# w_out in four pieces and a listed order anew: a linear-attention and gated feed-forward kernel on one core

## The chip, the cores and the metric

The kernel runs on one NeuronCore of a Trainium2 chip. Its engines are TensorE (PE in the profile, its weight loads PEld), VectorE (DVE), ScalarE (ACT), GpSimd (POOL) and SyncE (SP). Each works through its own list of instructions in order, and semaphores make one wait for another. SP and POOL also issue DMAs; all of them run on the core's 16 DMA engines. The metric is device time in microseconds of one execution, as a median over runs.

## The reference

Eight batches of eight heads, 576 tokens, head width 64, then a gated feed-forward over the 4608 tokens:

```python
q_s = exp(q - max(q, -1));  q_s = q_s / (sum(q_s, -1) + 1e-09)     # over the head width
k_s = exp(k - max(k, 2));   k_s = k_s / (sum(k_s, 2) + 1e-09)      # over the tokens
kv  = einsum('bhsd,bhse->bhde', k_s, v)
x   = einsum('bhsd,bhde->bhse', q_s, kv)     # then (4608, 512): tokens x heads * width
out = ((x @ w1) * (x @ w2)) @ w3 @ w_out     # 512 -> 1024, 1024 -> 1024, 1024 -> 512
```

q, k, v, the weights and the output are float32 in DRAM; the matmuls take float16.

## The kernel before

**The fold.** Nothing stands between w3 and w_out, so the kernel first forms W3O = w3 @ w_out (1024 x 512) and later multiplies by that alone. It does this in eight blocks of 128 rows of w3, `ft` 0 to 7 (`fold`, lines 411 to 442). For each block PE transposes eight 128 x 128 tiles (`w3t`), ACT or DVE copies them out of PSUM (`w3T`), PE multiplies them with w_out in eight matmuls of 512 columns that accumulate in one PSUM bank (`pf`), and ACT or DVE scales the sum into W3O (`W3O`). The eight matmuls are cut into as many steps as w_out has pieces: step `pf.ft.h` takes piece `h` alone, so it can start when that piece has landed.

**The attention** of batch b (`attention`). For k: the maximum over the tokens (`kmx`, `cb`), its subtraction (`ksub`, in two halves of the heads), the exponential (`kexp`), the product with v (`kv`, on PE) and its division by the sums (`kv2`). v of later batches is first cast (`vc`). For q, in two parts of the tokens: maximum (`qmx`), subtraction (`qsub`), exponential (`qexp`), sum (`qsm`), a small constant added (`qeps`), reciprocal (`qrc`), product (`qn`). Then q is transposed, for batches 0 and 1 on PE (`qt`, copied out by `qT`), for the others by a transposing DMA on SP (`qd`). PE multiplies it with kv (`xm`, `xt` for the last 64 tokens), and `xs` and `xts` copy the result out as x.

**The feed-forward** of chunk c (`chunk`): eight pairs of PE steps, `up.1` with w2 and `up.0` with w1; `bs` copies the first product out, `ab` multiplies the two on DVE; then four `down` steps with W3O, their copies `os` and the stores `st` on SP. Chunk 8 holds the last 64 tokens of all batches.

**The order.** Every step is named, and `ORDER` (lines 80 to 150) lists all of them. `Plan.run` (lines 51 to 75) emits them in that order, so each engine's and each queue's order is the list's, restricted to it. `PICKS` says which engine takes a step that has a choice; its names hold for the batches from 3 on together (`qeps_3_1`). Some DVE and POOL steps share a port; for the first `LINKED` places of the list the kernel adds a wait wherever the holder of that port changes engine. `FILL` puts matmuls on zeros ahead of a step: 17 at the beginning and 16 ahead of `pf.4.0`.

**The loads.** SP loads q of batch 0 (`HW`), and later what batches from 2 on need. POOL issues the loads in `LOADS` (lines 198 to 202): the weights, which are cast to float16 on the way, and k, v and q of the first batches. A load on POOL's queue waits until the load eight places ahead of it has landed (`load`, line 400). w3 comes in six pieces (`ROWS`: rows of blocks 0, 1, 2, 3, 4-5, 6-7), w1 and w2 in four (`COLS`). The number of w_out's pieces is this line (239), used by `side` and `fold`:

```python
    WOS = 2
```

Of the kernel before, what the change touches and what calls it, by code (L numbers as in the profile page):

```python
# [201 lines left out]
]  # L202
# [673 lines left out]
```

## Time and profile before

| | |
|---|---|
| median of three runs | 243.53 us (243.4 to 244.03) |
| the profiled execution, its own time | 243.27 us |
| its span in the trace | 241.5 us |
| PE busy | 234.5 us, 97% of the span |
| DVE, ACT, POOL busy | 170.8, 123.4, 124.0 us |
| PE's waits for DMAs | 2.2 us, in four places, all before 25.4 us |
| matmuls on zeros | 33, 10.0 us |
| DMA | 45.66 MB, a mean of 189 GB/s |

The span runs from the first to the last instruction in the trace; the execution's own time adds what lies around it. Times inside the trace are microseconds from the span's start. In a group's line an arrow `a<-b` says that a is written from b; `<-DMA v` behind a wait says that it was ended by a DMA that wrote v. In the timeline of an engine the first number is the start, the second the duration of a merged run of like instructions, and brackets hold the idle time before it.

### The profile page before, as it was taken

Reading aid. Unit: us, or ns where it says so; the run is one execution under the profiler, and the core shown is the slowest. Engines: PE = TensorE matmul, PEld = TensorE weight load, DVE = VectorE, ACT = ScalarE, POOL = GpSimd, SP = SyncE. Lnnn points to the kernel's source line nnn. Section 1 sums busy time; section 2 is a strip of 40 time slices with the busy share of each in tenths; the row PEclk is TensorE's granted clock in tenths of the full one; section 3 lists DMA queues with packets and bytes.
Section 4 is the critical chain, followed back from the end, with each engine's and each line's share of the span. In section 5 each row is a group of like instructions: output and inputs, shape, how many; then the busy total and the mean of one; then the engine's idle time right before and its main releaser. Section 6 shows DMA issues by size and latency. Waiting matters only on the chain.

```text
span 241.5 us, 4827 instructions
## 1 busy us (share of the span) xinstructions
PE 234.5 (97%) x1917; PEld 114.6 (47%) x1917; DVE 170.8 (71%) x293; ACT 123.4 (51%) x194; POOL 124.0 (51%) x79
## 2 busy tenths in 40 slices
...
PEclk9999999999999999999999999999999999999999
...
GB/s 209 310 209 250 305 302 200 249 370 356 399 388 160 274 1 114 380 341 83 206 400 124 248 401 281 153 0 35 165 76 3 49 38 133 0 0 0 88 132 130
DMA packets 37894, 45.66 MB, mean 189 GB/s; under 512 B 15984, under 2 KB 22384, under 8 KB 37872
## 3 DMA queue, kind: packets, MB, share of 16 engines
...
q0 software_dynamic: 7792, 11.14, 21.0%
...
q14 instruction: 7, 0.06, 0.1%
...
## 4 chain that ended last, share of the span: by engine, by line
PE 88%; DMA 7%; POOL 2%; issue 1%; ACT 0%; POOLq 0%
PE pab L735 52%; PE po L757 23%; DMA v<-in_v_dram 7%; PE po L772 3%; PE po L427 3%; PE pkv L515 2%; PE xm L621 2%; POOL w L377 1%; PE w3t L415 1%; PE xt L621 1%; PE pkv L524 1%; POOL wosb L377 0%; PE qtp L595 0%; POOL q L377 0%; POOL k L377 0%
## 5 line engine op out<-in xcount | busy, mean ns | idle before, releaser
L750 DVE TENSOR_TENSOR ab<-pab,bsb 128x512 f16<-128x512 f32 x72 | 48.8, 684 | 28.4 <-PE pab L735 24.8
L735 PE MATMUL pab<-x,w1sb 128*128 128x512 f16 (+1 forms) x288 | 65.9, 356 | 0.0
L735 PE MATMUL pab<-x,w2sb 128*128 128x512 f16 (+1 forms) x288 | 65.8, 356 | 0.0
L298 ACT CAST bsb<-pab 128x512 f16<-128x512 f32 x59 | 34.6, 586 | 52.0 <-PE pab L735 51.7
L757 PE MATMUL po<-W3O,ab 128*128 128x512 f16 x256 | 59.5, 380 | 0.0
L490 POOL TENSOR_TENSOR k<-k,cb 128x1152 f32<-128x1152 f32 x15 | 39.2, 2629 | 20.3 <-DVE cb L486 19.1
L735 PEld LDWEIGHTS <-w2sb 128*128 128x128 f16 x320 | 30.7, 98 | 30.6 <-issue 0.2
L735 PEld LDWEIGHTS <-w1sb 128*128 128x128 f16 x320 | 30.6, 98 | 29.6 <-issue 0.2
L580 POOL TENSOR_TENSOR en<-eq,qr 128x1280 f16<-128x1280 f16 (+1 forms) x15 | 32.1, 2141 | 15.3 <-ACT x L302 6.3
L757 PEld LDWEIGHTS <-ab 128*128 128x128 f16 x256 | 24.0, 98 | 29.2 <-issue 2.7
L548 POOL TENSOR_TENSOR q<-q,qm 128x1024 f32<-128x1024 f32 (+1 forms) x14 | 29.7, 2126 | 8.6 <-DVE qm L543 6.3
L298 ACT COPY osb<-po 128x512 f32<-128x512 f32 (+1 forms) x29 | 16.6, 572 | 28.5 <-PE po L757 22.6
L459 DVE TENSOR_REDUCE km<-k 128x128 f32<-128x1152 f32 x12 | 25.4, 2115 | 0.0
L543 DVE TENSOR_REDUCE qm<-q 128x20 f32<-128x1280 f32 (+1 forms) x16 | 21.4, 1344 | 4.1 <-DMA q<-in_q_dram 4.1
L302 ACT ACTIVATE x<-xm 128x512 f16<-128x512 f32 x30 | 16.5, 595 | 10.0 <-PE xm L621 9.8
L561 DVE TENSOR_REDUCE qr<-eq 128x20 f32<-128x1280 f16 (+1 forms) x16 | 21.3, 1330 | 0.4 <-ACT eq L556 0.4
L556 ACT ACTIVATE eq<-q 128x1280 f16<-128x1280 f32 (+1 forms) x16 | 18.6, 1165 | 5.6 <-POOL q L548 2.9
L498 ACT ACTIVATE ek<-k 128x1152 f16<-128x1152 f32 x16 | 18.5, 1164 | 2.5 <-POOL k L490 2.5
L298 DVE CAST bsb<-pab 128x512 f16<-128x512 f32 x13 | 9.0, 690 | 13.4 <-PE pab L735 13.3
L427 PE MATMUL po<-wosb,w3T 128*128 128x512 f16 x64 | 15.3, 379 | 1.2 <-DMA wosb<-in_moe_w_out_dram 1.2
L325 PE MATMUL po<-zero 128*128 128x512 f16 x33 | 10.0, 470 | 1.6 <-DVE zero L320 1.6
L427 PEld LDWEIGHTS <-w3T 128*128 128x128 f16 x64 | 5.8, 98 | 7.8 <-ACT w3T L298 1.2
...
## 6 DMA issues: line engine op xcount, KB each, us to landing
...
v<-in_v_dram POOLq DMA_DIRECT2D x2, 576.0 KB, 14.6
...
wosb<-in_moe_w_out_dram POOLq DMA_DIRECT2D x2, 512.0 KB, 12.1
```

The source lines that it names most:

```text
L298: return [(nc.scalar.copy if eng == "ACT" else engine[eng].tensor_copy)(out=out, in_=in_)]
L427: nc.tensor.matmul(st["pf", ft], lhsT=st["w3T", ft][:, gt, :], rhs=wosb[:, gt, :], start=(gt == 0), stop=(gt == N_FT - 1))
L459: dve.tensor_reduce(out=st["km", b][:, two(hp), :], in_=kb[:, two(hp), :, :].rearrange("p h j d -> p h d j"), axis=AX.X, op=ALU.max)
L490: return [engine[eng].tensor_tensor(out=kb[:, two(hp), :, :], in0=kb[:, two(hp), :, :], in1=st["cb", b][:, two(hp), None, :].broadcast_to( ...
L543: dve.tensor_reduce(out=st["qm", b][:, :, j], in_=qb[:, :, j, :], axis=AX.X, op=ALU.max)
L548: return [engine[eng].tensor_tensor(out=qb[:, :, j, :], in0=qb[:, :, j, :], in1=st["qm", b][:, :, j, None].broadcast_to([P, HH, n, D]), op ...
L556: nc.scalar.activation(out=st["eq", b, p], in_=qb[:, :, j, :], func=AF.Exp)
L561: dve.tensor_reduce(out=st["qr", b][:, :, slice(*PARTS[p])], in_=st["eq", b, p], axis=AX.X, op=ALU.add)
L580: return [engine[eng].tensor_tensor(out=st["en", b][:, j, :, :].rearrange("p j h d -> p h j d"), in0=st["eq", b, p], in1=st["qr", b][:, :, ...
L735: nc.tensor.matmul(st["p", one, c, sub, u][:, a * (t1 - t0):(a + 1) * (t1 - t0)], lhsT=w[:, ct, fb * P:(fb + 1) * P], rhs=x()[:, ct, t0:t1 ...
L750: dve.tensor_tensor(out=st["ab", c][:, nf * u:nf * u + nf, t0:t1], in0=cut(st["p", 0, c, sub, u]), in1=cut(st["bsb", c, sub, u]), op=ALU.mult)
L757: nc.tensor.matmul(st["po", c, tb], lhsT=st["ab", c][:, ft, tb * P:(tb + 1) * P], rhs=W3O[:, ft, :], start=(ft == 0), stop=(ft == N_FT - 1))
```

## The change

w_out is loaded in four pieces instead of two, and the fold's eight matmuls of a block become four steps of two. In `LOADS` the pieces 1 and 0 stand ahead of k of batch 0, the pieces 2 and 3 behind it; w3's piece with blocks 6-7 (`w3.5`) moves from behind v of batch 0 to ahead of q of batch 1. The dummy matmuls ahead of `pf.4.0` go from 16 to 8. `ORDER` and `PICKS` are newly listed: up to chunk 4 the steps stand in another order, from there on in the old one, and some steps change engine. `LINKED` goes from 191 to 211, since the list has more steps ahead of the same point. The computation is the same. Of `ORDER` the diff shows the places that follow: the beginning up to the first `up` steps, and the stretch from `kv.2` to the transposes of batches 2 and 3.

```diff
-LINKED = 191
+LINKED = 211
 ORDER = """
-q.0.1 q.0.0 w3.4 k.0 wo.0 wo.1 ident w3.3 w3.0 qmx.0.1 w3.1 q.1.0 qsub.0.1 qexp.0.1 qmx.0.0 w3t.5
-v.0 w3t.4 qsm.0.1 w3T.4 qsub.0.0 qeps.0.1 w3.5 qexp.0.0 kmx.0.0 w3T.5 w3.2 pf.4.0 qrc.0.1 cb.0
-qn.0.1 pf.5.0 pf.4.1 qsm.0.0 k.1 qt.0.8 W3O.4 w2.0 w3t.3 qeps.0.0 ksub.0.1 pf.5.1 w3T.3 w1.0
-qt.0.16 w3t.0 qrc.0.0 qT.0.8 qn.0.0 pf.3.0 kexp.0.1 pf.3.1 w3T.0 ksub.0.0 w3t.1 W3O.5 qt.0.0
-w3T.1 W3O.3 pf.0.0 qmx.1.0 pf.1.0 kexp.0.0 qT.0.0 pf.0.1 qT.0.16 qsub.1.0 k.2 kv.0 w2.1 W3O.0
-qexp.1.0 pf.1.1 w1.1 kv2.0 w3t.7 w2.2 qsm.1.0 w3t.6 w3T.7 xm.0.1 w1.2 w3t.2 xs.0.1.0 w3T.6 pf.7.0
-W3O.1 xs.0.1.1 pf.7.1 qeps.1.0 pf.6.0 w3T.2 W3O.7 v.1 kmx.1.0 xm.0.0 pf.6.1 xs.0.0.1 xs.0.0.0
-pf.2.0 w2.3 up.1.0.0.0 w1.3 qrc.1.0 up.0.0.0.0 cb.1 bs.0.0.0 qn.1.0 up.1.0.0.1 up.0.0.0.1
-bs.0.0.1 ab.0.0.0 ksub.1.0 qt.1.0 kmx.2.0 pf.2.1 qT.1.0 up.1.0.0.2 W3O.2 xt.0 bs.0.0.2 q.1.1
...
-up.0.1.0.0 ab.0.0.7 qsub.1.1 kexp.2.1 up.1.1.0.1 qmx.2.1 bs.1.0.0 up.0.1.0.1 bs.1.0.1 ab.1.0.0
-down.0.0 qsub.2.1 qexp.1.1 qmx.2.0 vc.2.0 ab.1.0.1 q.3 up.1.1.0.2 v.3 qsm.1.1 vc.2.1 up.0.1.0.2
-k.4 qexp.2.1 up.1.1.0.3 qsub.2.0 os.0.0 qsm.2.1 up.0.1.0.3 qeps.1.1 bs.1.0.2 kv.2 qrc.1.1
-qexp.2.0 ab.1.0.2 down.0.1 qn.1.1 kv2.2 bs.1.0.3 q.4 st.0.0 ab.1.0.3 down.0.2 os.0.1 qmx.3.1
-st.0.1 qt.1.8 os.0.2 qeps.2.1 qrc.2.1 qt.1.16 qsub.3.1 down.0.3 qsm.2.0 qT.1.8 st.0.2 qT.1.16
-qmx.3.0 xm.1.1 down.1.0 xs.1.1.0 qn.2.1 kmx.3.1 xs.1.1.1 up.1.1.1.0 vc.3.0 qeps.2.0 up.0.1.1.0
-qexp.3.1 qd.2.1 qrc.2.0 kmx.3.0 qn.2.0 xt.1 up.1.1.1.1 os.0.3 up.0.1.1.1 bs.1.1.0 xts.1.0
-qsub.3.0 qd.2.0 up.1.1.1.2 xts.1.1 bs.1.1.1 qsm.3.1 ab.1.1.0 os.1.0 down.1.1 bs.1.1.2 ab.1.1.1
-st.1.0 up.0.1.1.2 os.1.1 qmx.4.1 up.1.1.1.3 v.4 st.1.1 ab.1.1.2 up.0.1.1.3 bs.1.1.3 qeps.3.1
-st.0.3 xm.2.0 vc.3.1 ab.1.1.3 down.1.2 xs.2.0.1 cb.3 xs.2.0.0 qsub.4.1 qexp.3.0 xm.2.1 down.1.3
-xs.2.1.0 qrc.3.1 xs.2.1.1 qsm.3.0 ksub.3.1 qexp.4.1 up.1.2.0.0 up.0.2.0.0 qeps.3.0 bs.2.0.0
...
+q.0.1 q.0.0 w3.4 wo.1 wo.0 k.0 wo.2 wo.3 w3.3 qmx.0.1 ident qsub.0.1 qmx.0.0 w3t.4 w3.0 qexp.0.1
+w3t.5 qsub.0.0 w3T.5 qsm.0.1 w3T.4 w3.1 qeps.0.1 qrc.0.1 w3.5 qexp.0.0 qn.0.1 pf.4.0 q.1.0 pf.5.0
+qsm.0.0 qt.0.16 pf.5.1 v.0 qt.0.8 pf.4.1 kmx.0.0 qeps.0.0 qT.0.8 pf.5.2 w3.2 pf.4.2 k.1 pf.5.3
+pf.4.3 W3O.5 qrc.0.0 W3O.4 cb.0 w3t.3 qn.0.0 w3T.3 w3t.0 qT.0.16 pf.3.0 w2.0 w3T.0 ksub.0.1
+pf.3.1 w3t.1 w1.0 pf.3.2 ksub.0.0 pf.3.3 pf.0.0 W3O.3 qt.0.0 w3T.1 pf.0.1 qT.0.0 pf.0.2 kexp.0.1
+pf.0.3 w3t.7 qmx.1.0 pf.1.0 w3T.7 pf.1.1 pf.1.2 W3O.0 kexp.0.0 pf.1.3 qsub.1.0 w3t.6 pf.7.0 k.2
+kv.0 W3O.1 qexp.1.0 w2.1 w1.1 pf.7.1 w3T.6 kv2.0 pf.7.2 w2.2 w3t.2 qsm.1.0 xm.0.1 w1.2 pf.7.3
+xs.0.1.1 pf.6.0 qeps.1.0 xs.0.1.0 w3T.2 pf.6.1 v.1 pf.6.2 W3O.7 kmx.1.0 xm.0.0 pf.2.0 xs.0.0.0
+pf.2.1 w2.3 xs.0.0.1 pf.2.2 pf.6.3 pf.2.3 w1.3 W3O.6 up.1.0.0.0 qrc.1.0 W3O.2 cb.1 qn.1.0
...
+qmx.1.1 bs.0.0.7 up.1.1.0.0 ab.0.0.7 up.0.1.0.0 qsub.1.1 bs.1.0.0 qmx.2.1 kexp.2.0 up.1.1.0.1
+down.0.0 bs.1.0.1 qmx.2.0 qsub.2.1 qexp.1.1 ab.1.0.0 up.0.1.0.1 os.0.0 down.0.1 ab.1.0.1 st.0.0
+vc.2.1 qexp.2.1 qsm.1.1 q.3 qsub.2.0 up.1.1.0.2 kexp.2.1 v.3 qsm.2.1 up.0.1.0.2 os.0.1 k.4
+up.1.1.0.3 vc.2.0 qexp.2.0 kmx.3.0 st.0.1 down.0.2 bs.1.0.2 q.4 qeps.2.1 bs.1.0.3 qeps.1.1
+qrc.1.1 kv.2 os.0.2 qn.1.1 ab.1.0.2 up.0.1.0.3 qrc.2.1 kv2.2 down.0.3 ab.1.0.3 qt.1.8 qn.2.1
+qmx.3.1 qt.1.16 os.0.3 down.1.0 qT.1.8 kmx.3.1 qT.1.16 qsub.3.1 qd.2.1 xm.1.1 down.1.1 xs.1.1.1
+qsm.2.0 xs.1.1.0 qexp.3.1 qeps.2.0 up.1.1.1.0 qrc.2.0 qmx.3.0 qn.2.0 up.0.1.1.0 bs.1.1.0 qsm.3.1
+up.1.1.1.1 os.1.1 vc.3.1 xt.1 qd.2.0 up.0.1.1.1 xts.1.0 ab.1.1.0 bs.1.1.1 qsub.3.0 up.1.1.1.2
+xts.1.1 st.1.1 ab.1.1.1 up.0.1.1.2 qmx.4.1 bs.1.1.2 st.0.3 os.1.0 up.1.1.1.3 ab.1.1.2 st.1.0
+up.0.1.1.3 qsub.4.1 bs.1.1.3 qeps.3.1 xm.2.0 ab.1.1.3 st.0.2 down.1.2 xs.2.0.0 qrc.3.1 xs.2.0.1
+cb.3 v.4 qexp.3.0 xm.2.1 down.1.3 xs.2.1.1 xs.2.1.0 qsm.3.0 ksub.3.0 qexp.4.1 up.1.2.0.0 kmx.4.0
+up.0.2.0.0 qeps.3.0 bs.2.0.0 up.1.2.0.1 ksub.3.1 ab.2.0.0 xt.2 bs.2.0.1 up.0.2.0.1 os.1.3 xts.2.1
+kexp.3.0 up.1.2.0.2 ab.2.0.1 st.1.3 up.0.2.0.2 qrc.3.0 xts.2.0 bs.2.0.2 qn.3.0 kexp.3.1
+up.1.2.0.3 ab.2.0.2 qmx.4.0 up.0.2.0.3 bs.2.0.3 qn.3.1 vc.3.0 qd.3.0 up.1.2.0.4 os.1.2 up.0.2.0.4
+ab.2.0.3 vc.4.0 st.1.2 qsm.4.1 kv.3 qsub.4.0 bs.2.0.4 qd.3.1 up.1.2.0.5 ab.2.0.4 up.0.2.0.5
+bs.2.0.5 k.5 q.5 qexp.4.0 up.1.2.0.6 ab.2.0.5 up.0.2.0.6 qeps.4.1 bs.2.0.6 qrc.4.1 up.1.2.0.7
+kv2.3 qn.4.1 up.0.2.0.7 ab.2.0.6 bs.2.0.7 xm.3.1 ab.2.0.7 down.2.0 xs.3.1.1 vc.4.1 kmx.4.1 qd.4.1
+xs.3.1.0 xm.3.0 down.2.1 xs.3.0.1 cb.4 xs.3.0.0 up.1.3.0.0 os.2.1 os.2.0 up.0.3.0.0 qsm.4.0
+ksub.4.1 st.2.0 down.2.2 qeps.4.0 st.2.1 bs.3.0.0 qrc.4.0 qmx.5.0 up.1.3.0.1 v.5 qn.4.0 kexp.4.1
+up.0.3.0.1 qmx.5.1 bs.3.0.1 down.2.3 ksub.4.0 os.2.2 qd.4.0 ab.3.0.1 ab.3.0.0 up.1.3.0.2 kmx.5.0
+up.0.3.0.2 qsub.5.1 xt.3 up.1.3.0.3 xts.3.1 kexp.4.0 bs.3.0.2 up.0.3.0.3 ab.3.0.2 up.1.3.0.4 k.6
...
-    "begin": 17, "pf.4.0": 16,
+    "begin": 17, "pf.4.0": 8,
...
-    "w3T_1_": "DVE", "w3T_2_": "DVE", "w3T_3_": "ACT", "ksub_0_0": "POOL", "vc_0_0": "ACT",
-    "vc_0_1": "ACT", "qeps_0_0": "DVE", "qsub_0_1": "DVE", "xs_0_1_1": "ACT", "xts_0_0": "ACT",
-    "qT_1_16": "ACT", "vc_2_0": "ACT", "xs_2_0_1": "ACT", "vc_3_1": "POOL", "bs_0_0_0": "ACT",
+    "w3T_1_": "ACT", "w3T_2_": "DVE", "w3T_3_": "ACT", "ksub_0_0": "DVE", "vc_0_0": "ACT",
+    "vc_0_1": "ACT", "qeps_0_0": "ACT", "qsub_0_1": "POOL", "xs_0_1_1": "ACT", "xts_0_0": "ACT",
+    "qT_1_16": "ACT", "vc_2_0": "POOL", "xs_2_0_1": "ACT", "vc_3_1": "POOL", "bs_0_0_0": "ACT",
-    "qsm_0_0": "DVE", "qn_0_0": "DVE", "qT_0_0": "DVE", "qmx_0_1": "DVE", "qsm_0_1": "DVE",
-    "qeps_0_1": "ACT", "qn_0_1": "POOL", "qT_0_8": "ACT", "qT_0_16": "DVE", "xs_0_0_0": "ACT",
+    "qsm_0_0": "DVE", "qn_0_0": "POOL", "qT_0_0": "DVE", "qmx_0_1": "DVE", "qsm_0_1": "DVE",
+    "qeps_0_1": "DVE", "qn_0_1": "DVE", "qT_0_8": "ACT", "qT_0_16": "ACT", "xs_0_0_0": "ACT",
-    "qsm_1_1": "DVE", "qeps_1_1": "ACT", "qn_1_1": "POOL", "qT_1_8": "ACT", "xs_1_0_0": "DVE",
+    "qsm_1_1": "DVE", "qeps_1_1": "DVE", "qn_1_1": "POOL", "qT_1_8": "ACT", "xs_1_0_0": "ACT",
-    "qsub_2_0": "POOL", "qsm_2_0": "DVE", "qeps_2_0": "ACT", "qn_2_0": "POOL", "qmx_2_1": "POOL",
-    "qsub_2_1": "POOL", "qsm_2_1": "DVE", "qeps_2_1": "DVE", "qn_2_1": "POOL", "xs_2_0_0": "ACT",
+    "qsub_2_0": "POOL", "qsm_2_0": "DVE", "qeps_2_0": "DVE", "qn_2_0": "POOL", "qmx_2_1": "POOL",
+    "qsub_2_1": "POOL", "qsm_2_1": "DVE", "qeps_2_1": "ACT", "qn_2_1": "POOL", "xs_2_0_0": "ACT",
-    "qeps_3_1": "DVE", "qn_3_1": "POOL", "xs_3_0_0": "ACT", "xs_3_0_1": "ACT", "xs_3_1_0": "ACT",
+    "qeps_3_1": "ACT", "qn_3_1": "POOL", "xs_3_0_0": "ACT", "xs_3_0_1": "ACT", "xs_3_1_0": "ACT",
...
 LOADS = [
-    ("w3", 4), ("k", 0), ("wo", 0), ("wo", 1), ("w3", 3), ("w3", 0), ("w3", 1), ("q", 1, 0),
-    ("v", 0), ("w3", 5), ("w3", 2), ("k", 1), ("w2", 0), ("w1", 0), ("k", 2), ("w2", 1),
-    ("w1", 1), ("w2", 2), ("w1", 2), ("v", 1), ("w2", 3), ("w1", 3), ("q", 1, 1),
+    ("w3", 4), ("wo", 1), ("wo", 0), ("k", 0), ("wo", 2), ("wo", 3), ("w3", 3), ("w3", 0),
+    ("w3", 1), ("w3", 5), ("q", 1, 0), ("v", 0), ("w3", 2), ("k", 1), ("w2", 0), ("w1", 0),
+    ("k", 2), ("w2", 1), ("w1", 1), ("w2", 2), ("w1", 2), ("v", 1), ("w2", 3), ("w1", 3),
+    ("q", 1, 1),
 ]
...
-    WOS = 2
+    WOS = 4
```

More of the change, by code (lines that the diff above doesn't have):

```diff
@@ L128 @@
-ksub.6.0 ab.5.0.0 up.1.5.0.2 os.4.2 bs.5.0.1 up.0.5.0.2 st.4.2 bs.5.0.2 ab.5.0.1 up.1.5.0.3
-ab.5.0.2 ksub.6.1 kexp.6.0 bs.5.0.3 up.0.5.0.3 ab.5.0.3 up.1.5.0.4 qmx.7.1 up.0.5.0.4 bs.5.0.4
-kexp.6.1 up.1.5.0.5 ab.5.0.4 qsub.7.1 up.0.5.0.5 bs.5.0.5 qmx.7.0 up.1.5.0.6 ab.5.0.5 kv.6
-qsub.7.0 bs.5.0.6 qexp.7.1 up.0.5.0.6 kv2.6 up.1.5.0.7 ab.5.0.6 up.0.5.0.7 bs.5.0.7 qsm.7.1
-qexp.7.0 xm.6.0 down.4.3 xs.6.0.0 ab.5.0.7 qeps.7.1 qrc.7.1 xs.6.0.1 down.5.0 qsm.7.0 qn.7.1
-os.4.3 st.4.3 kmx.7.0 xm.6.1 os.5.0 down.5.1 xs.6.1.0 st.5.0 xs.6.1.1 qeps.7.0 qrc.7.0 qd.7.1
@@ new lines @@
+qd.5.1 xm.4.0 down.3.1 xs.4.0.0 st.2.2 cb.5 xs.4.0.1 q.6 up.1.4.0.0 v.6 up.0.4.0.0 bs.4.0.0
+ksub.5.1 qexp.5.0 up.1.4.0.1 ab.4.0.0 xt.4 os.3.0 up.0.4.0.1 qsm.5.0 vc.5.0 down.3.2 ksub.5.0
+bs.4.0.1 qeps.5.0 ab.4.0.1 kexp.5.1 up.1.4.0.2 qrc.5.0 up.0.4.0.2 bs.4.0.2 qn.5.0 kexp.5.0
+up.1.4.0.3 ab.4.0.2 xts.4.1 k.7 qmx.6.1 up.0.4.0.3 os.3.1 vc.5.1 qd.5.0 os.3.2 up.1.4.0.4 xts.4.0
+bs.4.0.3 qsub.6.1 kv.5 st.2.3 bs.4.0.4 ab.4.0.3 up.0.4.0.4 vc.6.0 kv2.5 st.3.0 up.1.4.0.5
+ab.4.0.4 qexp.6.1 q.7 up.0.4.0.5 qmx.6.0 st.3.1 up.1.4.0.6 bs.4.0.5 qsub.6.0 up.0.4.0.6 v.7
```

78 lines of the change are left out of this document (35 added, 43 removed), and 16 rows, old and new, of the table PICKS.

## The prediction

> **What bounds the kernel now.** I read the page first, for who is busy and at what clock; then TensorE's waits, its timeline, the DMA view of the first 50 us, and the landing of single loads.
>
> ```profile
> PE 234.5 (97%) x1917; PEld 114.6 (47%) x1917; DVE 170.8 (71%) x293; ACT 123.4 (51%) x194; POOL 124.0 (51%) x79
> ...
> PEclk9999999999999999999999999999999999999999
> ...
> PE 88%; DMA 7%; POOL 2%; issue 1%; ACT 0%; POOLq 0%
> ```
>
> TensorE (PE) is busy 97% of the span (DVE 71%, ACT and POOL 51%) at full clock, and the chain that ended last is 88% PE. Its useful work does not change in amount, so a change can only move PE's idle time and its dummy matmuls. How long PE waits for loads, and for which:
>
> ```profile
> PE po L427 <- DMA wosb<-in_moe_w_out_dram: 1.2, 2, 0.8
> PE w3t L415 <- DMA w<-in_moe_w_dram: 0.8, 1, 0.8
> PE pkv L515 <- DMA v<-in_v_dram: 0.2, 1, 0.2
> ```
>
> The last wait is 0.2 us for v; none comes later. When they fall (start and duration):
>
> ```profile
> 1.55 6.35 PE L325 MATMUL po<-zero 128*128 128x512 f16 x17 [1.55 <-DVE zero L320]
> 8.73 1.21 PE L415 MATMUL w3t<-ident,w 128*128 128x128 f16 x16 [0.83 <-DMA w<-in_moe_w_dram]
> 9.78 3.62 PE L325 MATMUL po<-zero 128*128 128x512 f16 x16
> 14.14 1.89 PE L427 MATMUL po<-wosb,w3T 128*128 128x512 f16 x8 [0.75 <-DMA wosb<-in_moe_w_out_dram]
> 16.48 1.02 PE L427 MATMUL po<-wosb,w3T 128*128 128x512 f16 x4 [0.45 <-DMA wosb<-in_moe_w_out_dram]
> ...
> 25.32 0.48 PE L515 MATMUL pkv<-v,ek 64*64 64x64 f16 x36 [0.16 <-DMA v<-in_v_dram]
> ...
> 27.72 1.21 PE L415 MATMUL w3t<-ident,w 128*128 128x128 f16 x16
> ...
> 34.51 1.03 PE L735 MATMUL pab<-x,w2sb 128*128 128x512 f16 x4
> ...
> 40.42 1.04 PE L735 MATMUL pab<-x,w1sb 128*128 128x512 f16 x4
> ```
>
> The fold's first matmul (14.14) stands behind 16 dummies (9.78) and 0.75 us of waiting; kv.0 starts at 25.32, the first up matmul at 34.51, the first with w1's second piece at 40.42. From 25.32 on PE has no gap. Which loads set that pace: the DMA view of the first 50 us, the chain of waits, and one load by itself (issue, time to landing).
>
> ```profile
> q0 software_dynamic: 7792, 11.14, 101.2%
> ```
> ```profile
> 8.97 16.22 DMA v<-in_v_dram
> ```
> ```profile
> L377 POOL DMA_DIRECT2D w1sb<-in_moe_w_dram x1: 750/750/750, 26.8 to 26.8; - x1
> ...
> DMA to landing us min/median/max: 13.3/13.3/13.3
> ```
>
> POOL's queue alone fills the 16 DMA engines for 50 us (101%; packets overlap a little). Its loads land one behind another in issue order, so a landing is the sum of the loads ahead. v of batch 0 lands at 8.97 + 16.2 = 25.2, w1's second piece at 26.8 + 13.3 = 40.1, 0.35 us before PE uses it. Read in the same way: w3 rows 4-5 8.65, k 11.7, w_out's halves 14.0 and 16.45, w3 rows 3, 0 and 1 17.7, 19.0 and 20.3, q 21.7, w3 rows 6-7 27.7.
>
> **The change, part by part.** The sum is made against the profiled execution's own 243.27 us (span 241.5 and 1.77 around it), 0.26 below the median, 243.53.
>
> *w_out in quarters.* The same bytes in four loads. A quarter has the shape of a w3 row (256 KB), and those land 1.27 apart. Ends: 4.74 / 4 = 1.19 each (nothing added), and 1.30 (the slowest row; 0.46 in all). I take 1.27: 4 x 1.27 - 4.74 = 0.34 us on every load behind. POOL issues two more DMAs of 0.55 us by 5.4 us, when its queue holds a backlog of over 8 us: nothing. In PE's fold, quarters split the same 64 matmuls.
>
> For that 1.27 row the Trainium skill (DMA: Bandwidth & Descriptors, "Anatomy of one DMA") fits about 2.0 us fixed per DMA; by estimate, if the queue paid it each time, two more loads would cost 4.0 us and not 0.34. The 1.27 us between whole loads speaks against that reading.
>
> *Two quarters ahead of k.* They land at 9.9 and 11.2, k at 14.2 (was 11.7). The fill falls from 16 to 8 dummies (1.8 us less), and the fold waits for its transposed w3 instead: qsub.0.1, now on POOL (2.34, the 1280-wide POOL rows), ends at 8.8, the exponential at 10.1, two w3T copies of 1.0 on ACT at 12.1. So the fold starts some 1.9 us earlier. But quarters 2 and 3 land at 15.5 and 16.7, w3 row 3 at 18.0 and row 0 at 19.3: PE stops about five times for 0.4 to 0.8 us, and what it did early is caught up at the transposes of row 0, 19.3 against 19.26 before, with the same work behind them. The early start is worth nothing there.
>
> *w3 rows 6-7 ahead of q and v.* Their 27.7 - 25.2 = 2.5 us now lie ahead of v, which lands at 25.2 + 2.5 + 0.34 = 28.0; kv.0 starts near 28.2, 2.85 later. PE reaches it at 27.4 (19.3, four w3t sets 2.0, three folds 5.2, a qt 0.45, a quarter 0.43), so v decides. For that PE has done more ahead of kv.0: 5.25 folds and 7 w3t sets instead of 4.5 and 5, which is 0.75 x 1.73 = 1.30 and the pair of sets at 27.72 (1.13), 2.43. Net +0.4 us; ends +0.05 (quarters free) and +0.7 (1.30 each, the pair at 0.98). From kv.0 to the up matmuls less filler is left, 2.75 folds and one w3t, but kv2 (0.96) and each pair of xs evictions (1.1) still have 1.4 us or more of it beside them. By the first use of w1's second piece the set of work done is the same as before: it comes at 40.8, its weights land at 40.4.
>
> *k later.* kmx starts at 14.6 (behind qsm.0.0), cb ends at 19.8, both ksub run on DVE (1.35 each; one took 2.63 on POOL), the exponentials end by 26.9: 1.1 us of cover under v. POOL's loads behind v wait for slots and for qn.0.0 (1.9) under a backlog of 13 us: nothing.
>
> *Picks and order from 50 us on.* vc.2.0 moves from ACT to POOL (1.15) ahead of qn.1.1, and a kmx of batch 3 (2.16 on DVE) ahead of qrc.1.1, so qn.1.1 ends near 65.8 (was 63.4). Its consumer qt.1.8 stands behind down.0.3 now and is reached near 67.0; kv.2, behind down.0.2, near 63.9, when vc.2.0 has ended at 61.9. Both are covered, by 1.2 and 2.0. On SP q.3 moves behind st.0.0 and is issued near 58 (was 56.52), while loads ahead of it land until 60; qmx.3.1 does not ask for it before 66. qn.2.0 waits for its sum behind more DVE reductions and ends near 73.2 (was 72.33). Its transpose lands 4.5 to 5.4 us later (minimum and median of five from 66 to 100 us), at 77.7 to 78.6; PE wants it at 78.45 + 0.4 = 78.85: nothing, with 0.2 to 1.1 us of cover. qd.3.1, now behind a store and the other transpose, has about the same. The other picks (qeps, os, bs, xs: 0.15 to 0.7 each) move between engines with idle time, beside a PE that has work. From batch 5 on the order is the old one.
>
> Sum: +0.4 us, 243.7 for an execution like the profiled one, 243.9 against the median. About 0.3% (0.7 us) is what this kernel's times can tell from no change; so this forecasts none.
>
> **Rivals.**
> *The transposes of batches 2 and 3 become PE's wait (slower).* For it: the cover is 0.2 to 1.1 us, and one of the five took 8.6. Against: that one stood behind loads, and fewer stores stand ahead of these. It decides once landing takes over 5.6 us; at 6.0, xm.2.0 and xm.3.1 lose 0.4 to 0.5 each: 244.8.
> *k is late.* If its exponentials slip more than 1.1 us past 26.9 on a crowded DVE, kv.0 follows them; 1 us beyond that gives 245.
> *PE's clock falls back.* At the start 17 matmuls took 6.35 us, and 16 took 3.62 later. After the change PE idles 2.6 us between 12.2 and 19.3. If the clock halved for as long as it took to rise at the start, some 5 us, 2.5 us of work is lost, less 0.6 of waiting for v: 245.8. Against: the clock row shows no drop after gaps of 0.83, 0.75 and 0.45. The Trainium skill (TensorE: Matmul & The Clock Gate, "What's actually happening") lets the clock drop after some 3.4 us of idleness. No gap here would be that long.
> *Each added load holds the queue for a whole round.* The shortest issue-to-landing on the page is 2.0 us, of a 256 KB store; two of those instead of 0.34 put v 3.7 later: 247.6. Against: the 1.27 spacing.
> *The early fold carries through (faster).* Then 1.9 us less: 241.6. Against: w1's second piece lands at 40.1 even with free quarters, and the work before it is the same, so at most 0.36 us is to be won unless the queue itself runs faster.
>
> **How the numbers follow.** Forecast 0.56 (0.53 within 0.3%, 0.03 slower); transposes 0.22 (0.06 within, 0.16 slower); k late 0.06, clock 0.05 and added loads 0.03, all slower; early fold 0.08 (0.05 faster, 0.03 within). So faster 0.05, within 0.62, slower 0.33. The range 243.2 to 245.4 takes in the ends of the early sum (243.6 to 244.2), the small gain, the transposes and k late; the clock, the added loads and the full gain, 0.13, stay outside, with the outer parts of the others.
>
> **What would show it.** Right: the fold starts near 12.2, PE stops several times for w_out and w3 until 19.4, kv.0 waits for v until 28.2, w1's second piece is first used near 40.8, and PE has no gap after. Wrong: kv.0 before 27.5 or released by ACT; a PE wait for qT near 78 or 98; matmuls 0.43 us apart after 12; a wait for w1sb near 40.

## The result and the profile after

The changed kernel takes 244.76 us (median of five, 244.33 to 245.34) against 243.53 us (243.36 to 244.03) for the kernel before: a ratio of 1.0048, 95% interval 1.0026 to 1.0069. Measured once more, on another chip, it was 245.15 against 243.49, a ratio of 1.0066 (1.0048 to 1.0085). So it is slower, by 1.2 to 1.7 us. The forecast was 243.9 in a range of 243.2 to 245.4: the time lies in the range, but the likeliest case, no measurable change, is not what happened. It was the rival of the transposes (244.8), and one thing more that no case held.

The page of the changed kernel, as before: busy time of the engines, the granted clock in tenths over 40 slices, and the shares of the chain that ended last.

```profile
PE 233.9 (96%) x1909; PEld 114.2 (47%) x1909; DVE 163.5 (67%) x276; ACT 129.5 (53%) x210; POOL 125.1 (51%) x82
...
PEclk9999999999999999999999999999999999999999
...
PE 80%; DMA 13%; DVE 3%; POOL 2%; issue 1%; ACT 0%; POOLq 0%; ACTq 0%; DVEq 0%
```

PE is busy for 233.9 us (234.5 before, with 8 dummies more), at full clock throughout. DMA's share of the chain is 13% instead of 7%: it now runs through the loads of k and v up to 27.9 us, and through a transpose later on.

TensorE's waits in the changed kernel, from the view of waits (engine, line, what it waited for, us in total, times, longest), in full (the first line is its start):

```profile
PE po L328 <- DVE zero L323: 1.6, 1, 1.6
PE w3t L418 <- DMA w<-in_moe_w_dram: 1.2, 3, 0.5
PE qtp L598 <- DVE en L583: 0.8, 1, 0.8
PE xm L624 <- DMA qT<-en: 0.7, 1, 0.7
PE pkv L518 <- DMA v<-in_v_dram: 0.4, 1, 0.4
PE po L430 <- ACT w3T L301: 0.4, 1, 0.4
PE po L430 <- DMA wosb<-in_moe_w_out_dram: 0.3, 1, 0.3
```

All but one lie in the first 28 us, as predicted. The one that does not is 0.7 us for qT. Where they fall, from TensorE's timeline (start, duration, in brackets the idle time before it and what ended that):

```profile
12.13 1.04 PE L430 MATMUL po<-wosb,w3T 128*128 128x512 f16 x4 [0.39 <-ACT w3T L301]
...
19.18 0.70 PE L418 MATMUL w3t<-ident,w 128*128 128x128 f16 x8 [0.52 <-DMA w<-in_moe_w_dram]
...
27.92 0.48 PE L518 MATMUL pkv<-v,ek 64*64 64x64 f16 x36 [0.41 <-DMA v<-in_v_dram]
...
35.50 1.03 PE L738 MATMUL pab<-x,w2sb 128*128 128x512 f16 x4
...
40.55 1.04 PE L738 MATMUL pab<-x,w1sb 128*128 128x512 f16 x4
...
79.33 0.41 PE L624 MATMUL xm<-qT,kv 64*64 64x512 f16 x4 [0.67 <-DMA qT<-en]
```

The fold starts at 12.13 (before 14.14), the transposes of w3 row 0 at 19.18 (before 19.26), kv.0 at 27.92, the first up matmul at 35.50, the first with w1's second piece at 40.55 (before 40.42). At this point the change has cost 0.13 us. Then xm.2.0, the first output matmul of batch 2, starts at 79.33 after 0.67 us of waiting; in the kernel before it started at 78.45 and did not wait. From there the distance stays at 0.9 to 1.0 us: PE ends at 239.21, before at 238.21.

The chain that ended last (start, us, what) names the step:

```profile
71.22 1.91 POOL en L583
...
73.15 6.13 DMA qT<-en
...
79.33 0.41 PE xm L624 x4
```

qn.2.0 (POOL en) ends at 73.13, its transpose is issued at 73.15 and lands 6.1 us later. In the kernel before the same transpose was issued at 72.61 and landed 5.4 us later, at 78.00.

PE's 0.99 us (in unrounded times) are not the whole of the 1.67 us between the two profiled executions (244.94 and 243.27). The rest is behind PE, in the last store. From the view of that store alone (duration in ns, first and last start; then issue to landing), first the changed kernel:

```profile
L768 SPq DMA_DIRECT2D out_dram<-osb x1: 332/332/332, 239.7 to 239.7; - x1
...
DMA to landing us min/median/max: 2.3/2.3/2.3
```

and the kernel before:

```profile
L765 SPq DMA_DIRECT2D out_dram<-osb x1: 332/332/332, 238.7 to 238.7; - x1
...
DMA to landing us min/median/max: 1.7/1.7/1.7
```

The last store landed 2.3 us after its issue instead of 1.7, 0.63 us later by the landings in the trace. The DMA view of this stretch shows a packet in the changed kernel that the kernel before does not have there (queue, packets, MB, share):

```profile
q1 hardware_dynamic: 317, 0.29, 35.6%
q14 instruction: 1, 0.01, 1.7%
```

It is one packet of 8 KB on a queue that carries instructions. In the trace it runs from 240.71 to 241.36 us. Eight packets of the store start only when it is over, one behind another, to 241.70, while all the others had finished at 241.04. The store's 128 KB go out in packets of 1 KB, so eight are a sixteenth of it: by their number and their times they are the share of the one DMA engine, of 16, that carried the instructions. The trace itself does not name the engines. So there are two things to explain: 0.67 us of waiting for a transpose, and 0.63 us of a packet at the very end.

### The profile page after: what moved, and what is told of

Its sections match the earlier page's. It is cut to its first block, busy times and chain, and to the rows that moved or that the text cites. A ratio compares the mean times of both kernels' runs of the same rounds, so it can differ in the third digit from the quotient of the medians.

```text
span 243.2 us, 4811 instructions
## 1 busy us (share of the span) xinstructions
PE 233.9 (96%) x1909; PEld 114.2 (47%) x1909; DVE 163.5 (67%) x276; ACT 129.5 (53%) x210; POOL 125.1 (51%) x82
## 4 chain that ended last, share of the span: by engine, by line
PE 80%; DMA 13%; DVE 3%; POOL 2%; issue 1%; ACT 0%; POOLq 0%; ACTq 0%; DVEq 0%
PE pab L738 49%; PE po L760 21%; DMA v<-in_v_dram 5%; DMA k<-in_k_dram 5%; PE po L775 3%; DMA qT<-en 3%; PE pkv L518 2%; PE xm L624 2%; PE po L430 2%; DVE km L462 1%; POOL en L583 1%; DVE qm L546 1%; PE xt L624 1%; PE pkv L527 1%; DVE qr L564 0%
## 5 line engine op out<-in xcount | busy, mean ns | idle before, releaser
L493 POOL TENSOR_TENSOR k<-k,cb 128x1152 f32<-128x1152 f32 x14 | 36.5, 2625 | 17.8 <-DVE cb L489 17.8
L583 POOL TENSOR_TENSOR en<-eq,qr 128x1024 f16<-128x1024 f16 (+1 forms) x15 | 31.6, 2110 | 19.5 <-DVE qr L576 15.2
L301 ACT COPY osb<-po 128x512 f32<-128x512 f32 (+1 forms) x35 | 19.9, 573 | 32.1 <-PE po L760 23.7
L551 POOL TENSOR_TENSOR q<-q,qm 128x1280 f32<-128x1280 f32 (+1 forms) x15 | 32.0, 2139 | 6.5 <-DVE qm L546 6.5
L305 ACT ACTIVATE x<-xm 128x512 f16<-128x512 f32 x32 | 17.6, 596 | 9.3 <-PE xm L624 9.3
L301 DVE CAST bsb<-pab 128x512 f16<-128x512 f32 x13 | 8.9, 688 | 12.8 <-PE pab L738 12.7
L430 PE MATMUL po<-wosb,w3T 128*128 128x512 f16 x64 | 15.8, 380 | 0.6 <-ACT w3T L301 0.4
L328 PE MATMUL po<-zero 128*128 128x512 f16 x25 | 8.7, 521 | 1.6 <-DVE zero L323 1.6
```

The costliest lines, as they stand in the source:

```text
L301: return [(nc.scalar.copy if eng == "ACT" else engine[eng].tensor_copy)(out=out, in_=in_)]
L430: nc.tensor.matmul(st["pf", ft], lhsT=st["w3T", ft][:, gt, :], rhs=wosb[:, gt, :], start=(gt == 0), stop=(gt == N_FT - 1))
L493: return [engine[eng].tensor_tensor(out=kb[:, two(hp), :, :], in0=kb[:, two(hp), :, :], in1=st["cb", b][:, two(hp), None, :].broadcast_to( ...
L551: return [engine[eng].tensor_tensor(out=qb[:, :, j, :], in0=qb[:, :, j, :], in1=st["qm", b][:, :, j, None].broadcast_to([P, HH, n, D]), op ...
L583: return [engine[eng].tensor_tensor(out=st["en", b][:, j, :, :].rearrange("p j h d -> p h j d"), in0=st["eq", b, p], in1=st["qr", b][:, :, ...
```

## The experiments

Two theories for the transpose. **Theory S**: the sum of batch 2 comes late on DVE, so qn.2.0 ends 0.8 us later and its transpose is issued late. **Theory Q**: the queue ahead of the transposes on SP is late, because q.3 is now listed behind st.0.0 and is issued only when that store's data is there (58.49 instead of 56.52). For the packet, **theory F**: it belongs to ACT's program. All ratios are against the kernel before on the same chip.

**The two halves apart.** The listed order and the picks were cut behind kv.1 (near 47 us). In the first kernel the start is the changed one and the rest is that of before:

```diff
-LINKED = 211
+LINKED = 209
...
 xts.0.1 up.0.0.0.5 bs.0.0.5 bs.0.0.4 kv.1
-ab.0.0.4 q.2 ksub.2.1 v.2 up.1.0.0.6 kv2.1 k.3
+q.2 ab.0.0.4 ksub.2.0 up.1.0.0.6 v.2 kv2.1 k.3
...
-    "vc_2_0": "POOL"
+    "vc_2_0": "ACT"
```

The second is the other way round: w_out in halves and the order of before up to kv.1, then the changed one.

> The changed kernel up to kv.1 (loads, quarters, order and picks), then the kernel before's order and picks. Both theories place the lost time late, so both expect: fold from 12.1, kv.0 at 27.9, w1's second piece first used near 40.55 (0.13 later than before), no wait of xm.2.0 for qT, a median of 243.5 to 243.9, +0.13 us in all. If the start costs more than its trace shows, the median is 244.3 or above.

> The early part alone once more, since the first profile of it was taken at half clock. Both theories: kv.0 at 27.8 to 28.0, w1's second piece first used 0.1 to 0.2 us later than before (40.42), no wait for qT at xm.2.0, a median of 243.3 to 243.8.

> The kernel before up to kv.1 (w_out in halves, fill 16), then the changed kernel's order and picks. Both theories expect xm.2.0 to wait for qT by 0.7 to 0.9 us (PE comes 0.13 earlier, the transpose lands as late as in the changed kernel, 79.2 to 79.3) and a median of 244.2 to 244.5. If the start is what costs, xm.2.0 doesn't wait and the median stays at 243.5.

The start alone took 243.45 us, ratio 0.9988 (0.9976 to 1.0), and 243.50 in the second measurement, 0.9998 (0.9989 to 1.0007). In the profile of the second measurement kv.0 starts at 27.84, xm.2.0 at 78.50 without a wait, PE ends at 238.33 (before 238.21). The changed start is worth nothing and costs 0.1 us, as its trace said.

The late half alone took 243.87 us (243.43 to 244.94), ratio 1.0017 (1.0004 to 1.0029): slower, but by 0.3 us, where both theories expected a wait of 0.7 to 0.9 and a median of 244.2 to 244.5. In its profile (an execution of 244.18 us) xm.2.0 starts at 79.21 without waiting for qT, which landed at 78.53: PE itself was late, partly by a wait of 0.29 us for qn.1.1 at 67.37. So this half alone is late at xm.2.0 too, but not by the same wait, and both theories missed here. The instruction packet came at 243.4, after the end.

**The stores behind q.4 again.** The changed kernel with SP's order of before at this place, nothing else:

```diff
-qmx.1.1 ... up.0.1.0.0 ... os.0.0 down.0.1 ab.1.0.1 st.0.0
+qmx.1.1 ... up.0.1.0.0 ... os.0.0 down.0.1 ab.1.0.1
 vc.2.1 qexp.2.1 qsm.1.1 q.3 qsub.2.0 up.1.1.0.2 kexp.2.1 v.3 qsm.2.1 up.0.1.0.2 os.0.1 k.4
-up.1.1.0.3 vc.2.0 qexp.2.0 kmx.3.0 st.0.1 down.0.2 bs.1.0.2 q.4 qeps.2.1
+up.1.1.0.3 vc.2.0 qexp.2.0 kmx.3.0 down.0.2 bs.1.0.2 q.4 st.0.0 st.0.1 qeps.2.1
```

> The changed kernel with the stores st.0.0 and st.0.1 moved behind the load q.4 on SP, as in the kernel before; nothing else. Theory Q (a backlog in SP's queue: q.3 waits for the store ahead of it, so q.4 lands at 75.4 instead of 72.6 and both transposes stand behind it): q.3 issued near 57, q.4 landed by 74.2, the transpose of qn.2.0 landed at 77.8 to 78.4, no wait of xm.2.0, a median 0.6 us under the changed kernel's. Theory S (the sum of batch 2 comes late on DVE, so qn.2.0 ends at 73.1 and its transpose is issued late): the wait stays at 0.5 to 0.7 us and the median does not move.

It took 243.55 us, ratio 1.0001 (0.9992 to 1.001): the whole loss is gone. Of the two things to explain it has neither: its last store lands 1.7 us after its issue (of that below), and TensorE's waits are, in full:

```profile
PE w3t L417 <- DMA w<-in_moe_w_dram: 1.7, 3, 0.9
PE po L327 <- DVE zero L322: 1.6, 1, 1.6
PE qtp L597 <- DVE en L582: 0.8, 1, 0.8
PE po L429 <- ACT w3T L300: 0.4, 1, 0.4
PE po L429 <- DMA wosb<-in_moe_w_out_dram: 0.3, 1, 0.3
```

There is none for qT. The transpose of qn.2.0 in this kernel:

```profile
L605 SPq DMA_TRANSPOSE qT<-en x1: 1233/1233/1233, 73.1 to 73.1; - x1
...
DMA to landing us min/median/max: 4.9/4.9/4.9
```

It is issued at 73.07, as late as in the changed kernel (73.15), and lands at 77.96, 1.3 us earlier. So the late sum is not the cause, which speaks for Q and against S. The 1.2 us that come back are the wait and the packet together, so the landing is the measure for the two theories, and not the time. q.3 was issued at 56.56 and q.4 landed at 72.25 (75.37 in the changed kernel).

**qn.2.0 earlier.** The other side of the same question: the changed kernel with its SP order, and the sum moved up.

```diff
-... ab.1.0.3 qt.1.8 qn.2.1 ...
+... ab.1.0.3 qsm.2.0 qeps.2.0 qrc.2.0 qt.1.8 qn.2.1 qn.2.0 ...
...
-qsm.2.0 xs.1.1.0 qexp.3.1 qeps.2.0 up.1.1.1.0 qrc.2.0 qmx.3.0 qn.2.0 up.0.1.1.0
+xs.1.1.0 qexp.3.1 up.1.1.1.0 qmx.3.0 up.0.1.1.0
```

> The changed kernel with qsm.2.0, qeps.2.0, qrc.2.0 and qn.2.0 listed earlier (the sum right behind ab.1.0.3, qn.2.0 right behind qn.2.1), so that qn.2.0 ends near 70.3 instead of 73.1; SP's order unchanged. Theory S: the transpose is issued near 72.3, right behind the other, lands at 77.7 to 78.4, the wait of xm.2.0 is gone, a median 0.6 us under the changed kernel's. Theory Q: q.4 still lands at 75.4 and both transposes stand behind it, so qT lands at 78.9 or later and the wait stays at 0.3 to 0.7 us.

It took 244.84 us, ratio 1.0055 (1.0042 to 1.0068): no gain. PE ends 0.46 us earlier than in the changed kernel, at 238.75, but the last store landed 2.7 us after its issue instead of 2.3, so the time does not measure the transpose either. The transpose:

```profile
L605 SPq DMA_TRANSPOSE qT<-en x1: 3020/3020/3020, 72.3 to 72.3; - x1
...
DMA to landing us min/median/max: 6.6/6.6/6.6
```

Issued 0.9 us earlier, it landed at 78.81, 0.47 earlier than in the changed kernel: 0.1 us before Q's bound and well behind what S expected. The issue itself took 3.0 us on SP and ended at 75.28, when q.4 landed (75.31). PE did not wait for qT here only because the moved sum held up an ab on DVE for 0.36 us. S falls as the main cause, though half of the earlier issue came through.

**One store only.**

```diff
-up.1.1.0.3 vc.2.0 qexp.2.0 kmx.3.0 st.0.1 down.0.2 bs.1.0.2 q.4 qeps.2.1
+up.1.1.0.3 vc.2.0 qexp.2.0 kmx.3.0 down.0.2 bs.1.0.2 q.4 st.0.1 qeps.2.1
```

> The changed kernel with the store st.0.1 alone moved behind q.4 on SP; st.0.0 stays ahead of q.3. Theory Q, sharpened: SP's issue of the transposes ends when the last transfer ahead of them has landed, and qT lands 3.0 to 4.0 us after that. q.4 then lands near 74.7 (a store of 0.65 us less ahead of it than the 75.4 of the changed kernel), the second issue ends by 74.8, qT lands at 77.8 to 78.8, xm.2.0 waits 0 to 0.2 us and PE's end is 0.4 to 0.7 earlier. If only the late issue of q.3 counts, the wait stays at 0.5 to 0.7.

It took 244.59 us, ratio 1.0041 (1.0029 to 1.0053). q.4 landed at 74.48, near the expected 74.7, but qT at 79.18, not by 78.8, and xm.2.0 still waited 0.36 us (PE came 0.2 us later than in the changed kernel). My expectation had a hole: st.0.1 behind q.4 is still ahead of the transposes, and landed at 75.22. What counts here is the last transfer ahead, whichever it is, and in this order it follows q.3's late issue. The times from the landings in the trace, in us (the last three kernels come further below):

| kernel | q.3 issued | last transfer ahead landed | second issue, from to | qT landed | wait of xm.2.0 |
|---|---|---|---|---|---|
| before | 56.52 | 74.53 | 72.61 to 74.70 | 78.00 | none |
| changed | 58.49 | 75.37 | 73.15 to 75.33 | 79.28 | 0.67 |
| changed, again | 58.48 | 75.18 | 73.15 to 75.15 | 79.12 | 0.52 |
| one store later | 58.70 | 75.22 | 73.36 to 75.20 | 79.18 | 0.36 |
| qn.2.0 earlier | 58.38 | 75.31 | 72.25 to 75.28 | 78.81 | none |
| both stores later | 56.56 | 73.59 | 73.07 to 74.31 | 77.96 | none |
| late half alone | 58.63 | 75.23 | 74.31 to 75.55 | 78.53 | none |
| both stores later, 16 dummies | 57.13 | 74.93 | 74.41 to 75.65 | 78.32 | none |
| both stores later, a pick on ACT | 56.45 | 73.45 | 74.19 to 76.39 | 77.78 | none |
| before, with the stores first | 61.73 | 79.20 | 76.41 to 79.25 | 81.15 | 1.21 |

In six rows the issue on SP ends within 0.2 us of the last landing ahead; in three it takes 1.23 to 1.24 us, the shortest seen; the pick on ACT fits neither. qT lands 3.5 to 4.4 us after the last transfer ahead in the first six rows, and 2.0 to 4.4 over all ten. Of the 1.28 us between before and changed, 0.84 is the queue; 0.44 lies behind it, which these runs don't explain.

Two rows judge the theories more sharply than the times do. With the late half alone and with the pick on ACT the transpose is issued 1.2 and 1.0 us later than in the changed kernel, and lands 0.75 and 1.5 us earlier: a late issue is not the cause. But the late half alone has a queue almost as late as the changed kernel's (75.23 against 75.37), and there qT comes in time. So moving the stores decides whether the transposes are late, as Q says; by how much is only in part explained.

**The same two stores, in the kernel before.** Nothing but SP's order is changed:

```diff
-... vc.2.0 ab.1.0.1 q.3 up.1.1.0.2 v.3 qsm.1.1 vc.2.1 up.0.1.0.2
-k.4 qexp.2.1 ... kv2.2 bs.1.0.3 q.4 st.0.0 ab.1.0.3 down.0.2 os.0.1 qmx.3.1
-st.0.1 qt.1.8 ...
+... vc.2.0 ab.1.0.1 up.1.1.0.2 qsm.1.1 vc.2.1 up.0.1.0.2
+qexp.2.1 ... kv2.2 bs.1.0.3 st.0.0 q.3 v.3 k.4 ab.1.0.3 down.0.2 os.0.1 st.0.1 q.4 qmx.3.1
+qt.1.8 ...
```

> The kernel before, with nothing changed but SP's order: st.0.0 ahead of q.3 and st.0.1 ahead of q.4, as in the changed kernel. Theory Q: q.3 is issued near 60, q.4 lands at 75 or later, the transposes behind it land at 78.3 to 79.3, xm.2.0 waits 0 to 0.85 us, a median 0.3 to 0.8 us above before. Theory S: qn.2.0 still ends at 72.3, so no wait and no change.

It took 247.19 us, ratio 1.0159 (1.0128 to 1.019), 3.7 us slower where I expected 0.3 to 0.8. The store now ahead of q.3 could be issued only at 60.43, so q.3 was issued at 61.73 (56.52 before) and landed at 67.66 (62.84 before). DVE's timeline shows the reader:

```profile
62.99 0.69 DVE L750 TENSOR_TENSOR ab<-pab,bsb 128x512 f16<-128x512 f32 x1
67.76 1.49 DVE L543 TENSOR_REDUCE qm<-q 128x20 f32<-128x1280 f32 x1 [4.07 <-DMA q<-in_q_dram]
```

In the order of before DVE reaches qmx.3.1 at 63.7 and stands still for 4.07 us until q.3 is there; everything behind it is late, and xm.2.0 then waits 1.21 us for qT. The direction is Q's, and S expected nothing; but the price is mostly that of another reader, so this run doesn't measure the transposes' share.

**The packet at the end.** The changed kernel was measured again:

> The changed kernel once more, to see which parts of its extra time come back. Theory Q: xm.2.0 waits for qT by 0.4 to 0.9 us again and the median is 244.3 to 245.0. A second part of its profile, an 8 KB packet of instructions on one of the 16 DMA engines at 240.7 us, held the last store's landing to 2.3 us after its issue (1.7 in the kernel before): if it belongs to this program it is there again, and the span is 0.6 us longer than PE's end explains; if it came by chance, the last store lands 1.7 us after its issue.

245.15 us. xm.2.0 waited 0.52 us, the packet came at 240.5, and the last store landed 2.3 us after its issue. It belongs to the program. The packets of this queue, and ACT's instructions in the trace, with the time of the last packet: before 301 (175.5), late half alone 318 (243.4, after the end), both stores later 321 (242.0, after the end); changed, changed again, qn.2.0 earlier and one store later all 322, and 240.5 to 240.7. The other kernels with 301 or 305 of ACT's instructions have their last packet at 176 to 182, and the one with both stores later and 16 dummies (321) at 242.8. POOL, DVE and SP do not sort the kernels in this way. The test: the kernel with both stores later, which has neither the wait nor the packet, with one pick moved to ACT.

```diff
-    "qeps_2_0": "DVE"
+    "qeps_2_0": "ACT"
```

> The changed kernel with both stores behind q.4 (as in the run with the stores later, 243.55 us) and one pick moved from DVE to ACT, qeps_2_0, so that ACT's program has as many instructions as in the changed kernel (322 in the trace, where the run with the stores later had 321). Theory F (the 8 KB packet of instructions belongs to ACT's program, and falls on the last store where ACT reaches its last instructions one place earlier): the packet comes within 0.5 us of the last store's data again, at 239.5 to 240.8, the last store lands 2.3 to 2.7 us after its issue instead of 1.7, PE's end stays near 238.3, and the median is 244.0 to 244.4. If the packet hangs on something else, it comes at 242 or later, the last store lands 1.7 us after its issue, and the median stays at 243.5.

It took 244.39 us, ratio 1.0022 (1.0007 to 1.0036), where its base stood at 1.0001. PE ends at 238.20 and waits for no qT. The DMA queues on its page (packets, MB, share) have, for this queue,

```profile
q14 instruction: 8, 0.07, 0.1%
```

and on the page of its base one packet less within the span:

```profile
q14 instruction: 7, 0.06, 0.1%
```

The last store of the kernel with the moved pick:

```profile
L767 SPq DMA_DIRECT2D out_dram<-osb x1: 332/332/332, 238.7 to 238.7; - x1
...
DMA to landing us min/median/max: 2.3/2.3/2.3
```

The packet came at 239.7 and the store landed 2.3 us after its issue. All of it is as theory F expected: an instruction of 0.3 us, moved to an engine that is half idle, costs 0.5 to 0.8 us at the other end of the kernel. That the packet carries ACT's instructions is inferred from the order above and from this test; the trace gives only its queue. The Trainium skill (DMA: Bandwidth & Descriptors, "Queues, rings and completion order") says that each DMA engine takes turns between its queues a packet at a time. The Trainium skill (DMA: Bandwidth & Descriptors, "Why a DMA increments its semaphore by 16 and not by 1") says that only the full count, to which every engine adds, means that all data has landed. The trace agrees: one packet of 0.65 us, a sixteenth of the store behind it, and a landing 0.63 us later.

**The split alone.** The kernel before with quarters in the places of the halves:

```diff
-    WOS = 2
+    WOS = 4
...
-    ("w3", 4), ("k", 0), ("wo", 0), ("wo", 1), ("w3", 3), ...
+    ("w3", 4), ("k", 0), ("wo", 0), ("wo", 1), ("wo", 2), ("wo", 3), ("w3", 3), ...
```

> The kernel before with w_out loaded and folded in quarters, in the places of the halves; nothing else. By the prediction's step each load behind lands 0.34 us later (ends 0 and 0.46): v at 25.5, w1's second piece at 40.4, just in time, and the median moves by 0 to 0.35 us. By the changed kernel's trace (w1's second piece at 40.1) it costs 0.2 or less and the median stays.

It took 247.75 us, ratio 1.0178 (1.0152 to 1.0204), 4.3 us slower where the prediction had 0.34, and 0.46 at most. The loads themselves are hardly later: w3 row 1 lands 11.63 us after the first load (11.56 before). POOL's timeline shows where the time went:

```profile
9.38 0.53 POOL L400 DMA_DIRECT2D w<-in_moe_w_dram  x1 [2.72 <-DMA w<-in_moe_w_dram]
12.37 0.77 POOL L400 DMA_DIRECT2D q<-in_q_dram  x1 [2.46 <-DMA k<-in_k_dram]
13.51 0.75 POOL L400 DMA_DIRECT2D v<-in_v_dram  x1 [0.36 <-DMA wosb<-in_moe_w_out_dram]
14.27 1.92 POOL L571 TENSOR_TENSOR q<-q,qm 128x1024 f32<-128x1024 f32 x1
```

POOL issues eight loads, and the ninth only at 9.38, when the first had landed (9.09); the tenth at 12.37, when the second had (12.09). In the kernel before v is the ninth, and qsub.0.0 follows it at 9.74. With two loads more, q and v stand ahead of qsub.0.0 as tenth and eleventh, and it starts at 14.27. ACT's exponential and with it the copy of w3T follow, and PE waits 3.2 us for that copy. This wait costs more than its length. The granted clock on the page, and from PE's timeline the matmuls behind the wait:

```profile
PEclk9985999999999999999999999999999999999998
```
```profile
18.24 3.60 PE L450 MATMUL po<-wosb,w3T 128*128 128x512 f16 x8 [3.18 <-ACT w3T L321]
```

By the clock records of the trace the granted clock was half from 16.83 to 23.66 us, and these eight matmuls took 3.60 us where eight took 1.89 in the kernel before. kv.0 starts at 30.37 instead of 25.32. Of these 5.05 us, 2.5 are more idle time of PE ahead of it (4.69 us instead of 2.19 from 8 us on), and the rest is the same work at the lower clock: PE is busy for 237.0 us instead of 234.5. The profiled execution took 248.60 us; all six had a mean granted clock of 0.984 to 0.993, the kernel before 0.998 or more.

Theory W, eight open loads for POOL's queue (the bound that the section on the kernel before names), gives a cheap test: q and v behind qsub.0.0.

```diff
-q.1.0 qsub.0.1 qexp.0.1 qmx.0.0 w3t.5 v.0 w3t.4 qsm.0.1 w3T.4 qsub.0.0 qeps.0.1
+qsub.0.1 qexp.0.1 qmx.0.0 w3t.5 w3t.4 qsm.0.1 w3T.4 qsub.0.0 q.1.0 v.0 qeps.0.1
```

> The kernel before with w_out in quarters in the places of the halves (as in the run with the split alone), and on POOL the loads q.1.0 and v.0 listed behind qsub.0.0 instead of ahead of it. Theory W (POOL keeps eight loads open: the ninth and tenth are issued only when the first and second have landed, 9.1 and 12.1, and with two loads more qsub.0.0 stood behind them until 14.27): qsub.0.0 starts near 9.9, kv.0 at 25.2 to 25.6 instead of 30.4, a median of 243.5 to 243.9. If instead the two loads cost the time on the queue itself, kv.0 and the median stay at 30 and 247.

244.78 us, ratio 1.0063 (1.0038 to 1.0088). qsub.0.0 started at 9.68, and 3 of the 4.3 us came back. In the profiles kv.0 starts at 26.46 instead of 30.37, later than the expected 25.2 to 25.6; of these 3.9 us some 2.5 are the clock, which stays full in this one. What is left has the same cause one step on: the next two loads hold POOL until their eighth predecessors have landed, qn.0.1 behind them starts at 16.30 (14.93 before), and PE waits 1.3 us for it:

```profile
PE qtp L618 <- POOL en L603: 1.3, 1, 1.3
```

In this kernel v lands 16.67 us after the first load (16.50 before) and w1's second piece 31.35 (31.37 before). So two loads more cost the queue 0.2 us or less, and the wrong place on POOL up to 4.3, about half of it through the clock.

**The early start.** Both stores later, and 16 dummies instead of 8 ahead of the fold:

```diff
-    "begin": 17, "pf.4.0": 8,
+    "begin": 17, "pf.4.0": 16,
```

> The changed kernel with st.0.0 and st.0.1 behind q.4 (as in the run with the stores later) and, besides, 16 dummy matmuls ahead of the fold instead of 8, so the fold starts 1.7 us later, near 13.9. If the early start is worth nothing (the prediction's step): the waits for qn, w_out and w3 up to row 0 (2.2 us in all) shrink by as much, row 0's transposes still start near 19.3, kv.0 near 27.9, a median of 243.5. If the early fold carries through: 1 to 1.7 us slower.

244.22 us, ratio 1.0026 (1.0016 to 1.0036); the kernel without the dummies had 1.0001. The point in question came as predicted: the fold starts at 13.37 and row 0's transposes at 19.23 (12.41 and 19.43 without). But 0.6 us are lost behind that. The load q.1.0 (batch 1, first part), issued at 12.7 in both, took 13.0 us to land instead of the 11.7 of the changed kernel; its reader on DVE holds up an eviction of the fold, and PE waits 0.42 us. In the trace a packet of another instruction queue, 16 KB and 0.95 us long, comes at 22.9 instead of the 24.9 of the kernel without the dummies, just ahead of q.1.0's last bytes, and the first and the last of the 16 engines finish q.1.0 1.83 us apart (0.57 for the load ahead of it). That the eight dummies, as more instructions of PE's program, drew this packet forward fits the times: the four other kernels with 16 dummies whose clock stayed full have it at 22.5 to 22.9, those with 8 at 24.0 to 24.9. It was not tested by itself.

**The sum.** Of the 1.67 us between the profiled executions, 0.67 is the wait for qT, 0.2 PE's later arrival there (0.13 of it from the start), 0.1 small shifts behind it, 0.63 the packet, together 1.6; moving the two stores back behind q.4 removes wait and packet and brings 243.55, and the packet alone, added to that kernel, costs 0.5 to 0.8.

## Why the prediction was right in part

**The early part was right, its sizes too large.** The fold started at 12.13 (predicted 12.2), row 0 came at 19.18 (19.3), kv.0 waited for v until 27.92 (28.2), w1's second piece was first used at 40.55 (40.8). The net of this part was put at +0.4 and is +0.13; the start alone has a ratio of 1.00. The term of the sum that was mis-sized is the 0.34 us for quarters: two more loads in the order of before cost 0.07 us at w3 row 1, 0.17 at v and nothing at w1's second piece. The Trainium skill's fixed 2.0 us per DMA (DMA: Bandwidth & Descriptors, "Anatomy of one DMA"), read as a price that the queue pays for each load, would have made 4.0 us by estimate; the trace does not bear that reading out. The rival by which each added load holds the queue for 2.0 us falls with it.

**"POOL issues two more DMAs ... nothing" was wrong as a step, though it came out at nothing.** The backlog hides a transfer, not an issue that has to wait: POOL's ninth issue waits for the first landing, and what is listed behind it waits too. The bound of eight was known; the step priced the two issues and not what stands behind them. The changed kernel escapes because it lists qsub.0.1 and qsub.0.0 ahead of the ninth load (6.63 and 9.51). In the order of before the same split costs 4.3 us, the fall of the clock included.

**The other rivals fell.** The granted clock stays at full speed through all of the changed kernel's span, over the stops between 12 and 19 us too, of which the longest lasted 0.80 us. But that rival's mechanism and its price are real: behind the stop of 3.18 us in the kernel with the split alone the clock was half for 6.83 us and 2.5 us were lost, near the "some 5 us" and 2.5 of the prediction. The exponentials of k held nothing up. And the early fold does not carry through: with the fold 1 us later, row 0's transposes started at the same time.

**The step that failed is the transpose: "lands 4.5 to 5.4 us later".** It landed 6.13 us later. That qn.2.0 ends near 73.2 was right (73.13), and PE's arrival at 78.66 was even a little earlier than the predicted 78.85. The duration was taken from the minimum and median of five, as though it were a property of the transpose; it depends on the queue ahead of it (0.84 of the 1.28 us by which qT landed later), and on something that stays open (0.44). And that queue was in the prediction's hands: "q.3 moves behind st.0.0 and is issued near 58" (58.49). I priced this by q.3's own reader, qmx.3.1, which indeed did not wait, and not by what stands behind q.3 on SP: v.3, k.4, q.4 and the two transposes. The rival had the right place and the right threshold, 5.6 us, and 244.8 as its time, partly by luck: xm.3.1, to which it gave half of its loss, did not wait, and the packet at the end makes up for it.

**The packet was in no case.** The picks were costed at nothing because they "move between engines with idle time". That holds for the time that they take, and not for the length of ACT's program.

**The cover was too thin for its weight.** The forecast let a cover of 0.2 to 1.1 us hang on a duration known only as five values, of which one was 8.6 and another 7.7, both over the 5.6 at which the rival decides. It set the one aside because it "stood behind loads"; so did this one.
